# The first 20 feed-forward steps in a written order, the decay of chunk 1 moved onto q, and one chunk's PV in plain float32

## The chip, the cores and the metric

One core of a Trainium2 chip runs the program. The metric is the device time of one execution in microseconds (us). The kernel before takes 504.51 us in the median of three runs (504.18 to 506.27). Engines are named as in the profile: PE is TensorE (PEld its weight loads), DVE VectorE, ACT ScalarE, POOL GpSimd, SP the engine that issues most DMAs.

## The reference

An mLSTM attention over 768 positions (2 batches of 8 heads, head size 40), then two gated feed-forward layers on 1536 tokens of width 320 with an inner width of 1536, all in float32:

```python
for t in range(S):                                   # attention, state C, n, m
    m_new = np.maximum(f_gate[:, :, t] + m, i_gate[:, :, t])
    f_stab = np.exp(f_gate[:, :, t] + m - m_new)
    i_stab = np.exp(i_gate[:, :, t] - m_new)
    C = f_stab * C + i_stab * einsum('bhd,bhe->bhde', vt, kt)
    n = f_stab * n + i_stab * kt
    h_tilde = einsum('bhde,bhe->bhd', C, qt)
    y[:, :, t] = sigmoid(o_gate[:, :, t]) * h_tilde / max(|n . qt|, 1)
x = y.transpose(0, 2, 1, 3).reshape(1536, 320)
x = (sigmoid(x @ w_gate) * (x @ w_val)) @ w_out      # layer 1
xn = x / sqrt(mean(x * x) + 1e-6) * rms_g
g = xn @ w_gate2                                     # layer 2
out = (g * sigmoid(g) * (xn @ w_val2)) @ w_out2
```

## The kernel before

**Attention.** The 768 positions are six chunks of 128. For a chunk c and a batch b, `a_s` multiplies k and q, `a_p` multiplies the scores by a decay factor, `a_pv` multiplies them with v (the part of the output from inside the chunk), `a_inter` multiplies q with the masked state `cm` of the chunk before (the part from the state) and scales it by `te`, `a_u` updates the state, `a_h` adds the two parts, applies the sigmoid of the output gate and divides, and `a_x` transposes the result into `xT`. A float32 number for TensorE's faster type is held as a rounded high part and a low remainder: hence `xT` (high, low), the weights `wg` and `wo`, and `h` (high, low). The factors of chunks 0 and 1 come from matmuls, those of later chunks from a scan (`a_f`). The PV of chunk 2 and earlier is plain float32; from chunk 3 (`PB = 3`) on, the scores and v are split into three bfloat16 pieces each (`split3`, `a_v`), and each head takes three bfloat16 matmuls.

**Feed-forward.** A layer's inner width is cut into 12 weight tiles f. A step is one chunk (256 tokens in layer 1, 512 in layer 2) with one tile: `moe` or `moe2` does 16 matmuls into the bank `g`, a sigmoid on ACT and a product on DVE make `h`, and `moe_out` or `moe2_out` multiplies `h` with the output weights into the `o` banks. `ORDER` lists the 24 steps of chunks 0 and 1; then come 48 steps of chunks 2 to 5 and 36 of layer 2. A step's `moe_out` stands one step behind it for chunks 0 and 1, two behind for later chunks (`SKEW`).

**Weights.** Tile f comes in 64-bit form (960 numbers on 128 partitions) by `load_w` into one of two buffers `wraw`. `conv_w`, `conv_1` and `conv_2` make float32 of it: two ACT passes (or one, with a shift on DVE) and three DVE passes of 960, 640 and 320 columns. `split_w` makes `wg`: three ACT copies for the high parts, then the remainders: one 64x128 subtraction on POOL, one 128x512 subtraction on DVE (`go = 1`) or two 128x256 on POOL (`go = 0`), and another 64x128 on DVE (`low`). For chunks 0 and 1 the output weights stay plain float32 in `wf`; `split_o` splits them for later chunks.

**Order.** Each engine runs its own list of instructions in order, and waits for semaphores of the others. What the code emits in the prologue and in the first `NPIN = 8` steps is kept in the order of the code on each engine (`pin`); the rest is placed by a scheduler that goes by the code's order as priority. `early(i)` holds the attention work and the weight conversions that stand behind steps 0 to 3, `at(t, ...)` those of later steps. Two `wraw` buffers mean that the load of tile f + 2 waits for `conv_2` of tile f; SP issues loads in order, so what stands behind a waiting load waits too.

Of the kernel before, what the change touches and what calls it, by code (L numbers as in the profile page):

```python
# [19 lines left out]
L = 128  # L20
# [12 lines left out]
NPIN = 8  # L33
# [4 lines left out]
C2S = (8, 10)  # L38
XF = (0, 0, 0, 0, 0, 0, 0, 0, 0, 0, 0, 0)
LW = 9  # L40
FILL = (1, 3, 0, -3, 0, 0, 5)
ORDER = '000011110101010101010101'
C1S = (-4, -2)
EV1 = (-1, 4, 5, 0, 5, 3, 4, 5, 5, 6, 6, 7, 8)
EV2 = (0, 3, 3, 2, 4, 3, 3, 5, 5, 5, 5, 7, 7)
S0 = -4
CV = 5
SG1 = (0,) * NF
SG2 = (0, 0, 0, 0, 0, 0, 0, 0, 0, 0, 0, 0)
SP = 4  # L50
# [8 lines left out]
PB = 3  # L59
# [9 lines left out]
def mlstm_moe_kernel(ctx, tc, gate_if, gate_s, qk, qg, tok, w1, w2, rms_g, cst, out):  # L69
    nc = tc.nc  # L70
    pool = lambda name, bufs=1, **kw: ctx.enter_context(tc.tile_pool(name=name, bufs=bufs, **kw))
# [72 lines left out]
    def conv_w(f, tag="wc", lo_dve=0, both=True, sg_act=0, dve=False):  # L144
# [59 lines left out]
    def sub(eng, out, a, b):  # L204
        eng.tensor_tensor(out=out, in0=a, in1=b, op=ALU.subtract)  # L205
# [16 lines left out]
    def split_w(f, go=0, oo=0, both=True, eng=None):  # L222
# [12 lines left out]
        def low():  # L235
            sub(nc.vector, t[64:128, 0, 2, :], r[0:64], t[0:64, 0, 2, :])
# [39 lines left out]
    fd = dp.tile([U * (NC - LOGS), L], F32, name="fd")  # L276
    one = p2.tile([128, 8, E], F32, tag="hs", name="one").rearrange("p h e -> p (h e)").bitcast(BF16)[0:U, 0:S1]
# [154 lines left out]

    def a_inter(c, b, tag="a"):
# [3 lines left out]
        for g, (h0, n) in enumerate(GROUPS):  # L437
            nc.tensor.matmul(out=ps[:, h0 * E:(h0 + n) * E], lhsT=q[0:n * D, g, :], rhs=cm[0:n * D, g, 0:n * E], start=True, stop=True)  # L438
# [3 lines left out]
    def a_pv(c, qd, tag="a", fill=0):  # L442
        b, o = qd // 2, 4 * (qd % 2)
        if c >= PB:
            ps = pv_t[c, qd] = bank(tag)
        else:
            if o == 0:
                pv_t[c, b] = bank(tag)
            ps = pv_t[c, b]
        p = p_t.pop((c, qd))  # L450
        v = v_of(c, b)
        for i in range(4):
# [8 lines left out]
            nc.tensor.matmul(out=ps[:, (o + i) * E:(o + i + 1) * E], lhsT=p[:, i, :], rhs=v[:, o + i, :], start=True, stop=True)  # L461
# [171 lines left out]
    at(10, lambda: nc.gpsimd.tensor_scalar(out=rmsg, in0=rmsg, scalar1=2.0 ** -16, scalar2=None, op0=ALU.mult))  # L633
# [5 lines left out]
    for f in range(NF):  # L639
        t = pos[1, 0, f]  # L640
        at(NF * NAT + f - 1, split_o, f, O1[f])
        if f >= 6:
            at(t - LW, load_w, w1, f)
        if f >= 4:
            at(t - CV, keep.add, f)
            at(t - CV, conv_w, f, "wc", L1[f], True, SG1[f])
            at(t - SP, split_w, f, G1[f], O1[f])
# [3 lines left out]
        assert t + 1 < 72 + f and SP < CV  # L651
# [53 lines left out]
    load_qk(1, 1)  # L705
    gates_r2()
# [25 lines left out]
    keep.update((0, 1, 2, 3))  # L732
# [6 lines left out]
    a_o(0, 1)  # L739
    a_u(0, 0, "a")  # L740
    load_tok(1, 0)
# [5 lines left out]
    x = x_t.pop(0).rearrange("p b h d -> p b (h d)")  # L747
    a_u(0, 1, "o0")
    load_w(w1, 2)
    load_tok(1, 1, False)  # L750
    gates_r5b()
    idle = bank("o3")
    busy(idle, *[512] * 3)
    xT_dup(xT[1, 0], 0, x[:, 0], "o2", False)()
    conv_w(1, "wc", 1, False)
    a_s(1, 0, "aa")
    xT_dup(xT[1, 0], 1, x[:, 1], idle)
    rest()
    gates_r5c()
    conv_1(1)  # L760
    conv_2(1)
    load_w(w1, 3)
    p.tensor_copy(out=ident4, in_=ident.unsqueeze(1).to_broadcast([128, 4, L]))
# [108 lines left out]
    done = 0  # L872
    after = ExitStack()

    def early(i):

        if i == 0:
            split_w(1, 1)
            a_s(1, 1, ("o2", "o3"))
            for qd in range(4):  # L880
                a_k(1, qd)
            a_p(1, 0)
            a_p(1, 1)
            conv_w(2)
        elif i == 1:
            a_inter(1, 0)
            load_qg(1, 1)
            load_w(w1, 4)
            split_w(2, 1)
            a_p(1, 2, p2.tile([128, 4, L], F32, tag="ft", name="p"))  # L890
            a_p(1, 3, p2.tile([128, 4, L], F32, tag="ft", name="p"))
            a_o(1, 0)
            a_o(1, 1)
            a_pv(1, 0)
            a_pv(1, 1)
            a_u(1, 0)
            conv_w(3)
            load_w(w1, 5)
        elif i == 2:
            a_h(1, 0)  # L900
            split_w(3, 1)
            a_inter(1, 1, "o2")
            a_pv(1, 2, "o3")
            a_pv(1, 3, "o3")
            a_u(1, 1, "a")
            a_x(1, 0, "a")
            a_h(1, 1)
        elif i == 3:
            a_x(1, 1, "o2")

    assert min(ev) >= 0, min(ev)
    for i in range(len(seq) + SKEW):
# [9 lines left out]
        if 0 <= i < len(seq):  # L922
# [3 lines left out]
            if i < NPIN:  # L926
                early(i)
        while 0 <= i and done < len(seq) and done <= i - (SKEW if seq[done][0] == 1 and seq[done][1] >= NAT else 1):
            layer, c, f = seq[done]
            (moe_out if layer == 1 else moe2_out)(c, f)  # L930
            done += 1
# [84 lines left out]
```

## Time and profile before

| | us |
|---|---|
| median of three runs | 504.51 (504.18 to 506.27) |
| the profiled execution | 505.04 |
| its span, from the first to the last instruction | 503.2 |
| PE busy | 485.2 |
| DVE / ACT / POOL busy | 303.1 / 222.5 / 210.0 |
| mean granted TensorE clock | 0.989 |

The page's time slices show PE at nine tenths or more from a quarter of the span to the end, except in a stretch before three fifths of it. The three other engines are busiest in the first quarter and again in that stretch, where the second layer's weights come in. A matmul's record can overlap that of the next, so a sum of records is more than the time they take; where a cost is needed, starts of neighbouring records are compared.

### The profile page before, as it was taken

How to read it: one execution, taken by the hardware profiler on the slowest of the kernel's cores; microseconds unless marked ns; L12 is line 12 of the kernel's file. 1: busy time of each engine (PE TensorE's matmuls, PEld its weight loads, DVE VectorE, ACT ScalarE, POOL GpSimd, SP SyncE). 2: the span in 40 equal slices, each digit the busy share in tenths (PEclk: the TensorE clock that was granted, in tenths of full speed). 3: DMA queues.
4: the chain of work that ended last, by engine and by line, in shares of the span. 5: the costliest groups of instructions: out<-in, count | busy, mean ns of one | idle time of the engine just before them, and what ended most of it. 6: DMA issues, size and time to landing. Idle time of an engine off the chain costs nothing.

```text
span 503.2 us, 8423 instructions
## 1 busy us (share of the span) xinstructions
PE 485.2 (96%) x3264; PEld 434.8 (86%) x3266; DVE 303.1 (60%) x564; ACT 222.5 (44%) x485; POOL 210.0 (42%) x238
## 2 busy tenths in 40 slices
PE   8988989899999999999999889999999999999997
PEld 5877869678899999999999778988888888888886
DVE  6899594993679586596779986622352222432223
ACT  3764653553434543455578666322252222432122
POOL 2733385451256364354249996332213222132221
PEclk9998989899999999999999999999999999999999
DMA  7763736721123232023444412000010000100001
GB/s 233 250 208 116 239 108 251 253 98 40 61 64 84 80 85 82 1 67 108 158 158 156 158 66 92 1 0 1 0 54 0 1 0 1 53 2 0 1 0 52
DMA packets 12557, 42.58 MB, mean 85 GB/s; under 512 B 1590, under 2 KB 4870, under 8 KB 12518
## 3 DMA queue, kind: packets, MB, share of 16 engines
q1 hardware_dynamic: 12278, 41.84, 24.8%
q8 instruction: 25, 0.41, 0.3%
q10 hardware_dynamic: 240, 0.22, 0.2%
q14 instruction: 14, 0.11, 0.1%
HBM read 40.05 MB, written 2.00 MB: 84 GB/s over the span
## 4 chain that ended last, share of the span: by engine, by line
PE 65%; DVE 5%; DMA 4%; POOL 3%; issue 2%; ACT 1%; POOLq 0%; ACTq 0%
PE g L804 13%; PE a L804 13%; PE o L856 12%; PE g L786 11%; PE o L831 6%; PE o L786 4%; DMA wraw<-in_w_dram 4%; PE o L828 2%; POOL h L205 1%; POOL wg L205 1%; DVE wg L205 1%; PE a L392 1%; PE a L457 1%; PE a L438 1%; PE a L470 1%
## 5 line engine op out<-in xcount | busy, mean ns | idle before, releaser
L786 PE MATMUL g<-xT,wg 128*128 128x256 f32 x912 | 131.2, 293 | 1.1 <-ACT gb L338 0.4
L786 PEld LDWEIGHTS g<-xT,wg 128*128 128x128 f32 x912 | 118.2, 193 | 7.2 <-issue 1.7
L205 POOL TENSOR_TENSOR ft<-p,fb 128x512 fp32r<-128x512 f32 x35 | 45.2, 1293 | 130.6 <-ACT fb L813 130.5
L807 DVE TENSOR_TENSOR p<-p,g 128x512 f32<-128x512 f32 x36 | 24.5, 686 | 91.0 <-ACT p L806 91.0
L205 POOL TENSOR_TENSOR h<-sig,h 128x256 fp32r<-128x256 f32 x48 | 44.9, 938 | 57.2 <-ACT h L795 56.0
L831 PE MATMUL o<-wo,h 128*128 128x320 f32 x288 | 52.0, 313 | 3.9 <-POOL h L205 3.8
L856 PE MATMUL o<-wo,fb 128*128 128x320 f32 x288 | 52.9, 310 | 0.0
L804 PE MATMUL g<-xT,wg 128*128 128x512 f32 x180 | 50.7, 393 | 0.1
L813 ACT ACTIVATE fb<-p 128x512 fp32r<-128x512 f32 (+1 forms) x37 | 22.8, 620 | 60.7 <-DVE p L812 54.5
L806 ACT ACTIVATE p<-g 128x512 f32<-128x512 f32 x36 | 21.3, 596 | 62.9 <-PE g L804 59.8
L831 PEld LDWEIGHTS o<-wo,h 128*128 128x128 f32 x288 | 43.2, 189 | 6.2 <-POOL h L205 5.1
L804 PE MATMUL a<-xT,wg 128*128 128x512 f32 x180 | 47.6, 390 | 0.0
L856 PEld LDWEIGHTS o<-wo,fb 128*128 128x128 f32 x288 | 45.6, 188 | 2.0
L804 PEld LDWEIGHTS a<-xT,wg 128*128 128x128 f32 x180 | 33.7, 188 | 6.9
L812 DVE TENSOR_TENSOR p<-p,a 128x512 f32<-128x512 f32 (+1 forms) x37 | 24.6, 671 | 22.6 <-PE a L804 22.5
L804 PEld LDWEIGHTS g<-xT,wg 128*128 128x128 f32 x180 | 32.5, 188 | 5.5 <-ACT xT L515 0.4
L828 PE MATMUL o<-wf,h 128*128 128x320 f32 x96 | 34.1, 481 | 2.9 <-DVE h L791 2.9
L786 PE MATMUL o<-xT,wg 128*128 128x256 f32 x240 | 34.7, 290 | 0.0
L788 ACT ACTIVATE sig<-g 128x256 f32<-128x256 f32 x57 | 21.5, 377 | 26.8 <-PE g L786 23.5
L205 POOL TENSOR_TENSOR wg<-wc,wg 128x256 fp32r<-128x256 f32 (+1 forms) x30 | 22.8, 771 | 24.2 <-ACT wg L209 22.4
L167 ACT ACTIVATE wraw<-wraw 128x960 f32<-128x960 f32 x23 | 25.2, 1097 | 14.1 <-DMA wraw<-in_w_dram 13.9
L856 PE MATMUL o<-wo,ft 128*128 128x320 f32 x144 | 31.4, 309 | 0.0
(258 smaller groups left out, 863.5 us busy)
## 6 DMA issues: line engine op xcount, KB each, us to landing
wraw<-in_w_dram SPq DMA_DIRECT2D x24, 960.0 KB
tok<-in_tok_dram SPq DMA_DIRECT2D x12, 488.0 KB
fb<-fd SPq DMA_DIRECT2D x16, 256.0 KB
raw<-in_qk_dram SPq DMA_DIRECT2D x24, 160.0 KB
out_dram<-xn SPq DMA_DIRECT2D x12, 160.0 KB
qg<-in_qg_dram SPq DMA_DIRECT2D x10, 180.0 KB
rmsg<-in_rms_g_dram SPq DMA_DIRECT2D x1, 160.0 KB
cs<-in_cst_dram ACTq DMA_DIRECT2D x1, 136.5 KB
```

The source lines that it names most:

```text
L167: nc.scalar.activation(out=hi.bitcast(F32), in_=hi.bitcast(F32), func=AF.Copy, scale=2.0 ** -111)
L205: eng.tensor_tensor(out=out, in0=a, in1=b, op=ALU.subtract)
L786: nc.tensor.matmul(out=g[:, m, :], lhsT=w[:, m, ws, :], rhs=x[xs // 3][:, xs % 3, :], start=(i == 0), stop=(i == 7))
L788: nc.scalar.activation(out=sg, in_=g[:, 0, :], func=AF.Sigmoid, scale=2.0 ** -8)
L804: nc.tensor.matmul(out=g[m], lhsT=w[:, m, ws, :], rhs=x[xs // 3][:, xs % 3, :], start=(i == 0), stop=(i == 7))
L806: nc.scalar.activation(out=sg, in_=g[0], func=AF.Sigmoid, scale=2.0 ** -8)
L807: nc.vector.tensor_tensor(out=sg, in0=sg, in1=g[0], op=ALU.mult)
L812: nc.vector.tensor_tensor(out=sg[:, n], in0=sg[:, n], in1=g[1][:, n], op=ALU.mult)
L813: nc.scalar.activation(out=h[0][:, n], in_=sg[:, n], func=AF.Copy)
L828: nc.tensor.matmul(out=o, lhsT=h[:, n], rhs=w, start=(f == 0), stop=(f == NF - 1))
L831: nc.tensor.matmul(out=o, lhsT=h[:, hs, n], rhs=w[:, ws, :], start=(f == 0 and i == 0), stop=(f == NF - 1 and i == 2))
L856: nc.tensor.matmul(out=o, lhsT=h[hs][:, n], rhs=w[:, ws, :], start=(f == 0 and i == 0), stop=(f == NF - 1 and i == 2))
```

## The change

The prologue and the first 20 steps (`NPIN = 20`) stand in a written order. Two tables, `pre` and `post`, list what is emitted ahead of and behind each step's `moe`; they take the place of `early` and of the entries of `at` for chunk 2 and for the weight tiles of layer 1. In parts:

- Chunk 1: `load_q1` loads q into the (still unused) weight buffers of tiles 10 and 11, `load_e` reads the decay `er` back from DRAM as a broadcast, and `a_q` multiplies q by it on POOL. The state part and PV then accumulate in one bank, so that scaling by `te` and adding the two parts fall away, and `a_h0` finishes the chunk.
- Chunk 3's PV is plain float32 (`PB = 4`), with 8 matmuls for a batch instead of 24, and without `split3` and the splitting of v.
- Weights: tile 1's shift moves from DVE to ACT (`conv_z`). For tiles 2 to 11 of layer 1 the remainders are all made on POOL (`go = 0`); `low` goes to POOL wherever `go = 0`, in layer 2 as well (tiles 2, 3, 6, 7, 9 and 11).
- The output of steps 0 to 2 stands behind the attention work of the same step; `gates_r5b` uses one bank; three dummy matmuls go; the scaling of `rmsg` moves from POOL to ACT; `split_o` and all that is not pinned stands behind step 19.

```diff
-NPIN = 8
+NPIN = 20
-C2S = (8, 10)
+C3S = (19, 25)
-ORDER = '000011110101010101010101'
+ORDER = '000011110101010101010011'
-PB = 3
+PB = 4
@@ split_w
         def low():
-            sub(nc.vector, t[64:128, 0, 2, :], r[0:64], t[0:64, 0, 2, :])
+            sub(nc.vector if go else nc.gpsimd, t[64:128, 0, 2, :], r[0:64], t[0:64, 0, 2, :])
@@ chunk 1
+        nc.sync.dma_start(out=ed, in_=er[:, 0:L])
+    def load_e(b):
+        t = eq_t[b]
+        for i in range(3):
+            n = 3 if i < 2 else 2
+            rows = ed[8 * b + i:8 * b + i + 3 * (n - 1) + 1:3, :]
+            nc.sync.dma_start(out=t[D * i:D * i + D, 0:n], in_=rows.unsqueeze(0).to_broadcast([D, n, L]))
+    def a_q(b):
+        q, t = qg_t[1, b], eq_t.pop(b)
+        for n, g in ((120, slice(0, 2)), (80, slice(2, 3))):
+            nc.gpsimd.tensor_tensor(out=q[0:n, g], in0=q[0:n, g], in1=t[0:n, g], op=ALU.mult)
@@ a_inter
-            nc.tensor.matmul(out=ps[:, h0 * E:(h0 + n) * E], lhsT=q[0:n * D, g, :], rhs=cm[0:n * D, g, 0:n * E], start=True, stop=True)
+            nc.tensor.matmul(out=ps[:, h0 * E:(h0 + n) * E], lhsT=q[0:n * D, g, :], rhs=cm[0:n * D, g, 0:n * E], start=(c > 1 or g == 0), stop=(c > 1))
+        if c == 1:
+            pv_t[c, b] = ps
+            return
@@ the written order
+    pre = {
+        0: [(a_p, 1, 0), (tile_b, 1)],
+        1: [(tile_d, 1), (tile_b, 2)],
+        2: [(a_h0, 0, 1), (tile_b, 3)],
+        3: [(tile_b1, 4), (a_x, 1, 1, "o2"), (tile_b2, 4)],
+    }
+    post = {
+        0: [(a_p, 1, 1), (tile_c, 1, 1), (tile_a, 2), (conv_z, 2), (a_s, 1, 1, ("o2", "o3")), ...
...
+        19: [(a_u, 2, 1), (lambda: nc.scalar.activation(out=rmsg, in_=rmsg, func=AF.Copy, scale=2.0 ** -16),)],
```

`tile_a` is ACT's part of a tile's conversion, `tile_b` DVE's and the load of tile f + 2, `tile_c` the split.

On DVE, at the start of the steps, stood this (`wc<-wraw` and `wf` are a tile's conversion, `wg` its remainders, `p` scores times decay, `h` a step's product, `hs<-a,te` the state part scaled):

```order
L205 TENSOR_TENSOR xT<-o_387,xT 128x3x128
L176 TENSOR_SCALAR wc<-wraw 128x960
L205 TENSOR_TENSOR xT<-o_383,xT 128x3x128
L205 TENSOR_TENSOR wg<-wc,wg 64x128
...
L791 TENSOR_TENSOR h<-sig,g 128x256
L205 TENSOR_TENSOR wg<-wc,wg 128x2x256
L205 TENSOR_TENSOR wg<-wc,wg 64x128
L401 TENSOR_TENSOR p<-a,d_195 128x512 x2
...
L791 TENSOR_TENSOR h<-sig,g 128x256
L440 TENSOR_TENSOR hs<-a,te 128x336
L205 TENSOR_TENSOR wg<-wc,wg 128x2x256
L205 TENSOR_TENSOR wg<-wc,wg 64x128
```

In the changed kernel the same place reads so:

```order
L208 TENSOR_TENSOR xT<-o_362,xT 128x3x128
L208 TENSOR_TENSOR xT<-o_403,xT 128x3x128
L406 TENSOR_TENSOR p<-a,d_196 128x512
...
L814 TENSOR_TENSOR h<-sig,g 128x256
L406 TENSOR_TENSOR p<-a,d_196 128x512
L208 TENSOR_TENSOR wg<-wc,wg 128x2x256
L208 TENSOR_TENSOR wg<-wc,wg 64x128
...
L814 TENSOR_TENSOR h<-sig,g 128x256
L406 TENSOR_TENSOR p<-o_473,d_197 128x512
L406 TENSOR_TENSOR p<-o_474,d_197 128x512
```

The gaps hold the passes of a tile's conversion. The shift, the remainders of tiles 2 and 3 and the scaling of `hs` are gone from DVE; the first scores times decay stand ahead of tile 1's conversion.

On POOL, near the end of layer 1, the remainders of layer 2's weights stand between the steps' `h`. Before:

```order
L205 TENSOR_TENSOR h<-sig,h 128x256 x2
L205 TENSOR_TENSOR wg<-raw,wg 128x256 x2
L205 TENSOR_TENSOR wg<-raw,wg 64x128
L205 TENSOR_TENSOR h<-sig,h 128x256
L205 TENSOR_TENSOR wo<-wc,wo 128x320
L205 TENSOR_TENSOR wo<-tok,wo 128x320
```

After:

```order
L208 TENSOR_TENSOR h<-sig,h 128x256
L208 TENSOR_TENSOR wo<-wc,wo 128x320
L208 TENSOR_TENSOR wg<-raw,wg 128x256 x2
L208 TENSOR_TENSOR wg<-raw,wg 64x128 x2
L208 TENSOR_TENSOR wo<-tok,wo 128x320
L208 TENSOR_TENSOR h<-sig,h 128x256
```

Between two `h` there now stand six subtractions in a row, where it was three and then two; one of them is the `low` that was on DVE.

## Rows read from the trace of the kernel before

**Rows 1.** Busy us by stretch, engine by engine, then granted clock, DMA share, GB/s
```profile
26.00:52.00 26.00, 22.92 (x163) 19.71 (x164) 25.11 (x50) 13.84 (x28) 7.28 (x12) 0.93 0.42 145
52.00:138.00 86.00, 80.57 (x546) 70.59 (x545) 60.48 (x98) 42.07 (x87) 40.15 (x48) 0.96 0.45 153
138.00:223.00 85.00, 85.00 (x766) 82.48 (x766) 62.42 (x142) 39.01 (x101) 45.60 (x58) 1.00 0.22 62
223.00:300.00 77.00, 72.76 (x578) 68.60 (x575) 64.45 (x113) 51.19 (x122) 49.14 (x50) 1.00 0.38 131
300.00:503.00 203.00, 199.59 (x1045) 175.51 (x1044) 70.94 (x122) 62.18 (x124) 54.73 (x48) 1.00 0.06 20
```

**Rows 2.** What PE waited for over the whole span: us in total, times, longest
```profile
PE o L831 <- POOL h L205: 3.8, 3, 1.8
PE o L828 <- DVE h L791: 2.9, 2, 2.3
PE a L438 <- DVE p L401: 2.0, 1, 2.0
PE a L553 <- DVE x L499: 1.7, 1, 1.7
```

**Rows 3.** A stretch of 2 us, columns as in rows 1
```profile
46.00:48.00 2.00, 2.00 (x6) 1.41 (x5) 1.93 (x7) 1.98 (x2) 0.99 (x2) 0.50 0.02 4
```

**Rows 4.** DVE's groups, 24 to 52 us: busy us, mean ns, idle before
```profile
L205 DVE TENSOR_TENSOR wg<-wc,wg 128x512 fp32r<-128x512 f32 x3 | 2.1, 685 | 0.0
L205 DVE TENSOR_TENSOR wg<-wc,wg 64x128 fp32r<-64x128 f32 x4 | 1.5, 378 | 0.1
L176 DVE TENSOR_SCALAR wc<-wraw 128x960 int32<-128x960 int32 x1 | 1.1, 1120 | 0.0
L440 DVE TENSOR_TENSOR hs<-a,te 128x336 f32<-128x336 f32 x1 | 0.5, 500 | 0.0
L490 DVE TENSOR_TENSOR hs<-a,hs 128x336 f32<-128x336 f32 x1 | 0.5, 494 | 0.0
```

**Rows 5.** POOL's groups of weight remainders, 60 to 303 us
```profile
L205 POOL TENSOR_TENSOR wg<-wc,wg 128x256 fp32r<-128x256 f32 x12 | 12.9, 1095 | 0.1
L205 POOL TENSOR_TENSOR wg<-wc,wg 64x128 fp32r<-64x128 f32 x9 | 4.2, 461 | 10.6 <-ACT wg L209 10.2
L205 POOL TENSOR_TENSOR wg<-tok,wg 64x128 fp32r<-64x128 f32 x3 | 2.6, 873 | 0.2
```

**Rows 6.** PE in order of time at two PVs: start, us, instruction, count
```profile
40.13 1.92 PE L461 MATMUL o<-tok,p 128*128 128x42 f32 x16
41.87 0.81 PE L470 MATMUL a<-tok,kk 128*120 128x126 f32 x6
...
139.61 1.02 PE L457 MATMUL a<-wraw,wc 128*128 128x42 bf16 x22
140.47 2.16 PE L786 MATMUL g<-xT,wg 128*128 128x256 f32 x16
```

**Rows 7.** POOL in order of time while layer 2's weights are split
```profile
281.72 3.27 POOL L205 TENSOR_TENSOR wg<-raw,wg 128x256 fp32r<-128x256 f32 x3 [1.01 <-ACT wg L209]
...
285.89 1.30 POOL L205 TENSOR_TENSOR wo<-wc,wo 128x320 fp32r<-128x320 f32 x1
287.14 1.80 POOL L205 TENSOR_TENSOR wo<-tok,wo 128x320 fp32r<-128x320 f32 x1
288.90 1.65 POOL L205 TENSOR_TENSOR h<-sig,h 128x256 fp32r<-128x256 f32 x1
```

**Rows 8.** PE in order of time, the starts of two neighbouring steps
```profile
54.40 2.32 PE L786 MATMUL g<-xT,wg 128*128 128x256 f32 x16
...
57.39 2.32 PE L786 MATMUL g<-xT,wg 128*128 128x256 f32 x16
```

**Rows 9.** One small DVE subtraction beside POOL work
```profile
93.09 2.49 DVE L205 TENSOR_TENSOR wg<-wc,wg 64x128 fp32r<-64x128 f32 x1
```

**Rows 10.** ACT waiting for a weight tile of layer 1
```profile
88.14 1.12 ACT L167 ACTIVATE wraw<-wraw 128x960 f32<-128x960 f32 x1 [2.51 <-DMA wraw<-in_w_dram]
```

More of the change, by code (lines that the diff above doesn't have):

```diff
@@ L276, in mlstm_moe_kernel @@
     fd = dp.tile([U * (NC - LOGS), L], F32, name="fd")
+    ed = dp.tile([U, L], F32, name="ed")
     one = p2.tile([128, 8, E], F32, tag="hs", name="one").rearrange("p h e -> p (h e)").bitcast(BF16)[0:U, 0:S1]
@@ L446, in a_pv @@
         else:
-            if o == 0:
+            if o == 0 and c != 1:
                 pv_t[c, b] = bank(tag)
@@ L731, in mlstm_moe_kernel @@
     a_pv(0, 1, "a")
[L732 removed]
+    keep.update(range(NF))
     conv_w(0, "wc", 2, False, 0, True)
@@ L747, in mlstm_moe_kernel @@
     x = x_t.pop(0).rearrange("p b h d -> p b (h d)")
+    low = xT_dup(xT[1, 0], 0, x[:, 0], "o2", False)
     a_u(0, 1, "o0")
     load_w(w1, 2)
+    load_e(0)
     load_tok(1, 1, False)
[L751 to L755, printed above, removed]
+    load_e(1)
+    gates_r5b("g")
+    low()
+    xT_dup(xT[1, 0], 1, x[:, 1], "o3")
     a_s(1, 0, "aa")
-    xT_dup(xT[1, 0], 1, x[:, 1], idle)
     rest()
[L759 to L763, printed above, removed]
+    a_q(0)
+    a_q(1)
+    conv_z(1)
     def pin(first):
@@ L871, in mlstm_moe_kernel, with ft_tile @@
     hst = {}
-    done = 0
     after = ExitStack()
[L875 to L909, printed above, removed]
+    def ft_tile():
+        return p2.tile([128, 4, L], F32, tag="ft", name="p")
@@ new lines, in tile_a, with tile_b, tile_b1, tile_b2 @@
+    def tile_a(f):
+        conv_w(f, "wc", 3, False)
+    def tile_b(f):
+        tile_b1(f)
+        tile_b2(f)
+    def tile_b1(f):
+        if f in tops:
+            conv_z(f)
+        conv_1(f)
+    def tile_b2(f):
+        conv_2(f)
+        if f + 2 < NF:
+            load_w(w1, f + 2)
+    lows = {}
+    def tile_c(f, go=0):
+        low = split_w(f, go, 0, not go)
+        if go:
+            lows[f] = low
+    def tile_d(f):
+        if f in lows:
+            lows.pop(f)()
+    pre = {
[4 more added lines that the diff above has]
+    }
@@ L911, in mlstm_moe_kernel, with do, out_steps @@
+    for f in range(4, NF):
+        pre.setdefault(2 * f - 3, []).append((tile_d, f))
+    def do(todo):
+        for fn, *args in todo:
+            fn(*(x() if x is ft_tile else x for x in args))
+    def out_steps(i):
+        nonlocal done
+        while 0 <= i and done < len(seq) and done <= i - (0 if done < 3 else SKEW if seq[done][0] == 1 and seq[done][1] >= NAT else 1):
+            layer, c, f = seq[done]
+            (moe_out if layer == 1 else moe2_out)(c, f)
+            done += 1
     assert min(ev) >= 0, min(ev)
@@ L925, in mlstm_moe_kernel @@
             (moe if layer == 1 else moe2)(c, f)
[L926 to L931, printed above, removed]
+        if i >= 3:
+            out_steps(i)
+        do(post.get(i, ()))
+        out_steps(i)
     after.close()
```

109 lines of the change are left out of this document (69 added, 40 removed).

## The prediction

> **What bounds the kernel now.** I read the page's time slices first, then PE's waits, then the busy time by stretch, then the engines in order of time where PE waits. From 300 us to the end PE is busy in 199.59 of 203.00 us, the rest being the tail behind the last matmul, and in 138 to 223 us it is busy in 85.00 of 85.00 us at a granted clock of 1.00 [rows 1]: there only less PE work saves time. It is fed badly in three stretches. From 26 to 52 us it is idle for 26.00 - 22.92 = 3.08 us while DVE is busy in 25.11 of 26; from 52 to 138 us idle for 86.00 - 80.57 = 5.43 us; from 223 to 300 us idle for 4.24 us [rows 1]. The first two have also a mean granted clock of 0.93 and 0.96 [rows 1]: after waits of 1.7 to 2.3 us [rows 2] PE goes on at the lower level (1.2 of 2.4 GHz) for some us, as at 46 us with a granted clock of 0.50 [rows 3]. Rows 2 name who is late: DVE with a product, with the scores and with x in the first two, and in the third POOL with `h`, three times, 3.8 us. So the front hangs on DVE's order and load, the third stretch on POOL's.
>
> **The sum.** It is made against the profiled execution, 505.04 us (span 503.2 and 1.8 around it), and put on the median of the runs, 504.51.
>
> *Prologue and steps 0 to 3 (26 to 52 us).* To be had: 3.08 us of waits and, from the clock, 0.07 x 26 = 1.8 us, together 4.9. DVE loses one shift of 1.12 us, two scalings of 0.50 and two additions of 0.49, two 128x512 remainders of 0.685 and two 64x128 of 0.378 [rows 4]: 5.2 us out of 25.11. So DVE, with no gap before, gets one of about 5 us, and x of chunk 1 comes before PE asks for it or less than 1 us later. The 1.7 us wait for x [rows 2], and the clock that falls after it, go. What is late next is the remainder of tile 2, now on POOL: 2 x 1.095 + 2 x 0.461 = 3.1 us behind ACT's copies [rows 5], against some 1.1 us on DVE, and PE's fifth matmul of the step reads the last of them. I leave 0.9 us of wait there and 0.7 us at x of chunk 1, so the credit is 4.9 - 1.6 = 3.3. Bounds: all goes, 4.9; or both tiles' longer chains (2 x 2.0) show in full and the clock falls again, a loss of 1.
>
> The decay on q is four POOL multiplications ahead of tile 1's remainder. No row has their shape; a 64x128 subtraction took 0.46 and a 128x256 one 1.1 [rows 5], so four take 1.8 to 4.4, and since three quarters of them are nearer to the smaller in columns I take 2.5. They end about 30 us, and tile 1's remainder is asked for about 31: hidden by the first step's 16 matmuls (2.32 us [rows 8]) and the scores behind it. If their DRAM round trip is late (six broadcasts stand on SP behind two token loads and one weight load), PE waits at the state part up to 2 us; these 2 stand in the bound. The two q loads replace two that are gone; ACT takes the 1.1 us pass of tile 1 and the scaling of `rmsg`, with 13.84 us busy out of 26 and 42.07 out of 86 [rows 1]. The three dummy matmuls stood in a wait; their going is counted at nothing.
>
> *Steps 4 to 23 (52 to 138 us).* To be had: 5.43 us of waits and 0.04 x 86 = 3.4 us of clock, 8.8 in all. The 2.0 us wait for scores and the 2.3 us one for a product [rows 2] come from DVE's order: the wanted instruction stood behind weight conversions and scans. In the written order each `h` has at most a tile's conversion and one scan ahead of it, and its PE step starts two groups later; steps are 57.39 - 54.40 = 2.99 us apart [rows 8]. DVE loses the 128x512 remainders of tiles 9 to 11 and all `low`; POOL makes seven tiles at 3.1 us, 22 us, in a stretch in which it is busy in 40.15 of 86 us [rows 1], and of that its eight `wo` remainders leave for later. A weight tile is asked for every second step, 6 us, and has its conversion four steps ahead. I credit 6.4 and leave 2.4 (waits that an order by hand keeps). Bounds: 8.8 and 2.
>
> *What leaves this stretch* is the splitting of the output weights, pressed into some ten steps after step 19. ACT's 39.01 and POOL's 45.60 of 85 us [rows 1] cover it, and chunk 3 gives back ACT, DVE and POOL work there; without that cover it would cost a wait of about one `h`, 1 to 2 us, and it is part of the range.
>
> *Chunk 3's PV.* 22 of a batch's 24 bfloat16 matmuls take 140.47 - 139.61 = 0.86 us, so 24 take 0.94; the float32 ones of a batch take 41.87 - 40.13 = 1.74 us [rows 6]. PE pays 0.8 us for each of two batches where it has no slack: +1.6. All that ACT, DVE and POOL save in chunk 3 lies beside a PE that does not wait, and saves nothing.
>
> *Layer 2's weights (223 to 300 us).* The stretch moves earlier as a whole, since its first load waits for a buffer that PE's own progress frees. Inside it POOL gets `low` of tiles 2 and 3 (0.46 each) and of 6 and 7 (0.87 by the nearest row) before PE's last wait [rows 5]: 2.7 us on the engine that PE waits for. Also the order: between two `h` now stand both `wo` (1.30 and 1.80 us) and the `wg` group of 3.27 [rows 7] plus a `low`, some 7 us, where 3.1 us between two `h` already went with a wait of 1.8 [rows 2, 7]. Against it DVE gets free of four subtractions, and the `h` that is late had two steps, 6 us, of room. I charge 2.3. Bounds: 6 (both gaps show), and a gain of 1 (DVE's relief shows).
>
> Sum: -3.3 - 6.4 + 1.6 + 2.3 = -5.8. From 505.04 that is 499.2, and on the median **498.7 us**.
>
> **Where a page speaks against it.** Beside other POOL work a DVE subtraction of 64x128 took 2.49 us [rows 9] and 0.378 in the mean elsewhere [rows 4]: DVE stood still while POOL worked. The Trainium skill (SBUF — State Buffer, section Terms) says that the two share a pair of memory ports which one instruction holds to its end while the other is blocked. By that, moving remainders from DVE to POOL frees no time while both read memory; the trace agrees in rows 9. The time that this would give is the first rival.
>
> **Rivals.**
>
> 1. *DVE and POOL take turns, and the written order only shifts the waits.* If DVE stands still in every POOL remainder, steps 0 to 3 gain nothing (5.2 us off DVE, 2 x 3.1 us of POOL and 2.5 for q in its place), and of the 8.8 half is kept: 4.4. Then -4.4 + 1.6 + 2.3 = -0.5: 504.0. For it: rows 9. Against it: POOL is busy in only 7.28 of 26 us [rows 1], and in 24 to 52 us the 64x128 subtraction's mean is 0.378 [rows 4], so most of them went undisturbed.
>
> 2. *Nothing is late any more.* 4.9 + 8.8, less 1.6, with the third stretch as before: 504.5 - 12.1 = 492.4. For it: PE's own work is short enough, and 138 to 223 us shows that a full PE is possible. Against it: POOL's new load in the third stretch.
>
> 3. *Slower: the weights' loads become the bound.* A tile's load goes out only after the conversion of the tile two before it, and with 19 steps fixed nothing can be pulled ahead of ACT when it waits. ACT waited 2.51 us for a tile [rows 10]. If each of tiles 5 to 11 comes that late with the next sigmoid behind it on ACT, PE loses 7 x 2.5 = 17.5 us, against 9.7 of credit and with 3.9 of charges: 504.5 + 11.7 = 516. It decides once a load takes longer than the three steps, 9 us, from its issue to its use. Against it: in 52 to 138 us DMA is busy 0.45 of the time [rows 1], so there is room.
>
> **How the numbers follow.** What a measurement of this kernel can tell from no change is 0.5%, 2.5 us: 502.0 to 507.0. The forecast has 0.64, with its own range of 495 to 502; rival 1 has 0.15, rival 2 0.14, rival 3 0.07. Faster is nearly all of the forecast and rival 2, 0.76; same is rival 1, 0.15; slower is rival 3 and the outer end of the POOL charge, 0.09. The range takes in rival 2's edge and rival 1: 492.5 to 504.5.
>
> **What would show it.** Right: in 26 to 138 us of the changed kernel's time no PE wait over 1.5 us, a granted clock of 0.98 or more, and layer 1's first split output about 9 us earlier; PV of chunk 3 as 16 float32 records with 1.7 us to what follows; PE's waits for POOL's `h` near the end of layer 1 at 5 to 7 us in total, up from 3.8. Wrong: PE waits for `wg` from POOL in steps 1 to 3 for more than 3 us in all; ACT waiting for `wraw` in steps 5 to 18; or waits for `h` over 9 us, which would give back the front's gain.

## The result, and the profile after

The changed kernel takes 501.13 us in the median of 7 runs (497.9 to 513.47), the kernel before 504.78 us in 7 runs beside it. The ratio is 0.9916, with a 95% interval of 0.989 to 0.9943: faster by 0.8%. The prediction was 498.7 us, with 492.5 to 504.5 as its range. The profiled execution took 500.93 us, with a span of 499.1, against 505.04 and 503.2 before.

Some executions of most kernels here run at a lower clock throughout; the ratios leave them out and the medians do not, so where the two disagree, as in e5, the ratio counts.

What PE waited for over the span of the changed kernel, as in [rows 2]: us in total, times, longest.

```profile
PE o L854 <- POOL h L208: 4.3, 3, 2.8
PE o L851 <- DVE h L814: 1.9, 1, 1.9
PE a L397 <- issue: 1.6, 1, 1.6
...
PE o L582 <- DVE x L541: 0.5, 1, 0.5
```

The wait for the scores (2.0) is gone, that for chunk 1's x has shrunk (1.7, now 0.5), and one for a product of DVE's stays (2.3, now 1.9). One is new, 1.6 us ahead of the score matmuls of `a_s`. POOL's `h` costs 4.3 where it cost 3.8.

Busy time by stretch, with the columns of [rows 1]; the borders behind 52 us are moved with the work. The first row is a stretch of 2 us.

```profile
24.00:26.00 2.00, 2.00 (x18) 1.53 (x18) 0.56 (x1) 1.52 (x5) 1.71 (x4) 0.57 0.95 343
...
26.00:52.00 26.00, 24.87 (x184) 22.11 (x183) 21.52 (x40) 14.24 (x28) 15.42 (x22) 0.90 0.44 149
52.00:126.00 74.00, 70.47 (x486) 61.34 (x485) 50.97 (x78) 34.43 (x68) 37.62 (x56) 0.98 0.51 162
...
223.00:296.00 73.00, 68.68 (x542) 65.68 (x542) 59.42 (x95) 47.81 (x111) 48.01 (x49) 0.98 0.36 126
```

PE's idle time, read as stretch less busy, is 1.13 us in 26 to 52 (before 3.08), 3.53 in 52 to 126 (before 5.43 up to 138) and 4.32 in 223 to 296 (before 4.24) [rows 1]. Against that, the clock column is worse in two places: 0.90 instead of 0.93 in 26 to 52, and 0.57 just ahead of it. A clock of 0.90 over 26 us costs about 0.10 x 26 = 2.6 us, 0.57 over 2 us another 0.9. The front's waits went as planned and most of the gain was given back there in clock.

Two places explain the waits that are left. The first, DVE in order of time around 88 us:

```profile
85.02 1.64 DVE L193 SCALAR_TENSOR_TENSOR wc<-wraw,wc 128x960 int32<-128x960 int32 x1 [0.56 <-ACT wc L184]
86.69 2.00 DVE L205 SCALAR_TENSOR_TENSOR wc<-wraw,wc 128x640 int32<-128x640 int32 x1
88.61 0.48 DVE L205 SCALAR_TENSOR_TENSOR wf<-wraw,wc 128x320 int32<-128x320 int32 x1
89.01 0.49 DVE L518 TENSOR_TENSOR hs<-a,hs 128x336 f32<-128x336 f32 x1
...
94.32 1.16 DVE L193 SCALAR_TENSOR_TENSOR wc<-wraw,wc 128x960 int32<-128x960 int32 x1
95.51 0.82 DVE L205 SCALAR_TENSOR_TENSOR wc<-wraw,wc 128x640 int32<-128x640 int32 x1
```

and PE there:

```profile
87.52 0.48 PE L397 MATMUL a<-raw 40*128 40x128 f32 x2
89.61 1.13 PE L397 MATMUL a<-raw 40*128 40x128 f32 x14 [1.60 <-issue]
```

The profile puts the 1.60 us down to "issue". What PE stands for is a bank: `a` is held by PV until the addition of L518 has read it, that addition stands in the written order behind tile 9's conversion (the first three rows), and PE goes on 0.6 us behind the addition's start. The conversion was itself late: its first two passes took 1.64 and 2.00 us beside a POOL that ran without a gap from 84.96 to 88.01, and 1.16 and 0.82 for the next tile (the last two rows). These 1.66 us are about PE's wait, so by this estimate a DVE held up beside POOL is behind it, as in the second place.

The second is ahead of step 20's output, directly behind the last written step. DVE:

```profile
110.11 1.39 DVE L359 TENSOR_TENSOR_SCAN ft<-fb,ident 128x512 f32<-128x512 f32 x1
111.42 4.49 DVE L521 TENSOR_TENSOR x<-x,hs 128x320 f32<-128x320 f32 x1
...
115.90 0.41 DVE L814 TENSOR_TENSOR h<-sig,g 128x256 f32<-128x256 f32 x1
```

POOL in the same time:

```profile
109.73 0.69 POOL L506 TENSOR_TENSOR cm<-C,cs 120x252 f32<-120x252 f32 x1 [2.57 <-DVE C L505]
110.37 1.28 POOL L507 TENSOR_TENSOR cm<-C,cs 80x84 f32<-80x84 f32 x1
111.61 0.75 POOL L420 TENSOR_TENSOR vv<-tok,tg 128x336 f32<-128x336 f32 x1
112.32 0.46 POOL L436 TENSOR_TENSOR kk<-tok,ft 128x160 f32<-128x160 f32 x1
112.74 0.87 POOL L208 TENSOR_TENSOR wo<-wf,wo 128x320 fp32r<-128x320 f32 x1
113.57 0.75 POOL L420 TENSOR_TENSOR vv<-tok,tg 128x336 f32<-128x336 f32 x1
114.28 0.46 POOL L436 TENSOR_TENSOR kk<-tok,ft 128x160 f32<-128x160 f32 x1
114.70 0.86 POOL L208 TENSOR_TENSOR wo<-wf,wo 128x320 fp32r<-128x320 f32 x1
116.14 0.86 POOL L208 TENSOR_TENSOR wo<-wf,wo 128x320 fp32r<-128x320 f32 x1 [0.58 <-ACT wo L212]
```

The addition L521 takes 0.49 us at other places. Here it takes 4.49: POOL runs eight instructions with no gap from 109.73 to 115.56, and the addition ends 0.35 us after POOL's first pause. The product `h` that PE wants is queued two places behind it, so PE waits 1.93 us:

```profile
116.36 2.48 PE L851 MATMUL o<-wf,h 128*128 128x320 f32 x4 [1.93 <-DVE h L814]
```

Behind that wait the clock is low, and the output's four matmuls take 2.48 us, where with the clock up they take 1.3.

The same stood in the kernel before. The `h` that PE waited 2.3 us for there came directly behind the subtraction of [rows 9], which took 2.49 us beside POOL where the mean in 24 to 52 us is 0.378 [rows 4]:

```profile
95.60 0.42 DVE L791 TENSOR_TENSOR h<-sig,g 128x256 f32<-128x256 f32 x1
```

### The profile page after: what moved, and what is told of

Its sections match the earlier page's. It is cut to its first block, busy times and chain, and to the rows that moved or that the text cites. A ratio compares the mean times of both kernels' runs of the same rounds, so it can differ in the third digit from the quotient of the medians.

```text
span 499.1 us, 8348 instructions
## 1 busy us (share of the span) xinstructions
PE 484.7 (97%) x3246; PEld 436.3 (87%) x3247; DVE 284.0 (57%) x519; ACT 217.6 (44%) x475; POOL 218.6 (44%) x264
## 5 line engine op out<-in xcount | busy, mean ns | idle before, releaser
L809 PE MATMUL g<-xT,wg 128*128 128x256 f32 x912 | 128.4, 292 | 0.6 <-POOL wg L208 0.6
L830 DVE TENSOR_TENSOR p<-p,a 128x512 f32<-128x512 f32 x36 | 24.5, 687 | 90.9 <-ACT p L829 90.9
L208 POOL TENSOR_TENSOR wg<-wc,wg 64x128 fp32r<-64x128 f32 (+1 forms) x53 | 37.3, 715 | 31.9 <-ACT wg L212 27.1
L827 PE MATMUL a<-xT,wg 128*128 128x512 f32 x180 | 50.8, 394 | 0.1
L829 ACT ACTIVATE p<-a 128x512 f32<-128x512 f32 x36 | 21.3, 598 | 62.2 <-PE a L827 58.4
L827 PE MATMUL g<-xT,wg 128*128 128x512 f32 x180 | 47.4, 390 | 0.0
L827 PEld LDWEIGHTS a<-xT,wg 128*128 128x128 f32 x180 | 32.5, 188 | 5.5 <-ACT xT L544 0.4
L835 DVE TENSOR_TENSOR p<-p,g 128x512 f32<-128x512 f32 (+1 forms) x37 | 24.6, 672 | 21.3 <-PE g L827 21.2
L851 PE MATMUL o<-wf,h 128*128 128x320 f32 x96 | 31.3, 449 | 1.9 <-DVE h L814 1.9
L809 PEld LDWEIGHTS o<-xT,wg 128*128 128x128 f32 x240 | 31.1, 192 | 0.1
```

The costliest lines, as they stand in the source:

```text
L809: nc.tensor.matmul(out=g[:, m, :], lhsT=w[:, m, ws, :], rhs=x[xs // 3][:, xs % 3, :], start=(i == 0), stop=(i == 7))
L827: nc.tensor.matmul(out=g[m], lhsT=w[:, m, ws, :], rhs=x[xs // 3][:, xs % 3, :], start=(i == 0), stop=(i == 7))
L829: nc.scalar.activation(out=sg, in_=g[0], func=AF.Sigmoid, scale=2.0 ** -8)
L830: nc.vector.tensor_tensor(out=sg, in0=sg, in1=g[0], op=ALU.mult)
L835: nc.vector.tensor_tensor(out=sg[:, n], in0=sg[:, n], in1=g[1][:, n], op=ALU.mult)
L851: nc.tensor.matmul(out=o, lhsT=h[:, n], rhs=w, start=(f == 0), stop=(f == NF - 1))
```

## The experiments

Twelve kernels were run, each against runs of the kernel before on the same chip.

**e1, the changed kernel again**, beside the next three as their yardstick. No edit.

> The changed kernel once more, as the yardstick for the others of this call. By the theory of the clock (the small matmuls of the prologue, without the three dummy matmuls, let the granted clock fall to 0.5 for some 7 us before the first step): most of the runs at 501 us, and single ones near 498 us with a mean clock near 0.993, where that fall does not come. By the rival (the spread has another cause): the time varies without the mean clock varying with it.

500.69 us, ratio 0.9895 (0.9847 to 0.9943). Its six executions run from 497.18 us at a mean clock of 0.997 to 520.42 at 0.949, each lower clock with a longer time, so the rival is out; that the missing dummy matmuls are the cause is not shown by this. Its profiled execution is 2.8 us shorter than the first (span 496.3), and it is worth setting the two side by side, because the instructions are the same, the longer waits too, and the clock is not. One wait of 0.50 us, for `eq`, is in e1 and not in the first, where PE came there later. PE's waits of e1 between 24 and 126 us (one of 0.60 us for split weights is left out):

```profile
29.17 0.90 PE L463 MATMUL a<-cm,eq 120*128 120x126 f32 x6 [0.50 <-POOL eq L456]
...
44.85 0.41 PE L582 MATMUL o<-cs,x 128*128 128x128 f32 x2 [0.53 <-DVE x L541]
...
87.03 1.33 PE L397 MATMUL a<-raw 40*128 40x128 f32 x14 [1.60 <-issue]
...
115.28 1.34 PE L851 MATMUL o<-wf,h 128*128 128x320 f32 x4 [1.93 <-DVE h L814]
```

and three stretches of e1, columns as above:

```profile
24.00:32.00 8.00, 7.50 (x72) 6.57 (x72) 6.33 (x10) 5.78 (x12) 4.85 (x10) 1.00 0.80 256
...
85.00:95.00 10.00, 8.40 (x55) 7.61 (x55) 6.93 (x13) 3.81 (x7) 3.00 (x6) 0.83 0.67 208
...
116.00:120.00 4.00, 4.00 (x29) 3.27 (x28) 3.36 (x6) 1.32 (x3) 0.88 (x1) 1.00 0.00 0
```

In the first execution the clock was low in 24 to 31 us and after 116 us, and full after 88. In e1 it is full in 24 to 32 and after 116, and 0.83 after the wait at 87. From the wait for x to the one for the bank both executions take 42.18 us; from there to the wait for `h` 26.75 us in the first and 28.25 in e1. So the same wait of 1.6 us was followed by a low clock in one execution and not in the other, and the low clock cost 28.25 - 26.75 = 1.5 us there.

**e2, dummy matmuls.** The prologue gets dummy matmuls back, 2 x 512 columns ahead of each half's transposes.

```
+    idle = bank("o3")
+    busy(idle, 512, 512)
...
+    busy(idle, 512, 512)
```

> The change, with four dummy matmuls of 512 columns back in the prologue: two in PE's 0.46 us wait for x and two ahead of the second half's transposes, about 0.5 us of work on PE's path. Theory (clock): the granted clock stays at 1.00 from 24 to 32 us; the first step's 16 matmuls take 2.2 to 2.5 us in place of 3.7, and of the 2.8 us lost there 1.5 to 2.5 come back, since the decay on q and tile 1's remainder on POOL, which end at 33 us, are next to be late: 498.5 to 499.5 us. Rival (PE is held in this place by its operands, and the slow records only show that): no gain, 501 to 501.5.

498.36 us, ratio 0.9861 (0.9827 to 0.9896), with a full clock in 20 to 126 us in its profile. Its interval overlaps that of e1. The five executions in its ratio have mean clocks of 0.990 to 0.997; of the eleven in the ratios of the result and of e1 four reach 0.990. e7 and e10 below take up the question.

**e3, layer 2's `low` back on DVE.**

```
-            sub(nc.vector if go else nc.gpsimd, t[64:128, 0, 2, :], r[0:64], t[0:64, 0, 2, :])
+            sub(nc.vector if go or f in second else nc.gpsimd, t[64:128, 0, 2, :], r[0:64], t[0:64, 0, 2, :])
```

> The change, with the low remainder of layer 2's tiles back on DVE (as before the change); layer 1 as changed. Theory (these subtractions lengthen POOL's chain between two h): PE's waits for h near the end of layer 1 fall from 4.3 us to 3 to 4, and the clock does not fall there: 1 to 2 us less than the change, 499.5. Rival (the order between the two h counts, or DVE gives back what it gained): waits of 4 us or more and a time within 0.7 us of the change.

499.22 us, ratio 0.9861 (0.9817 to 0.9906). PE's waits for POOL's `h` in e3:

```profile
PE o L857 <- POOL h L210: 2.6, 2, 1.8
```

That is 1.7 us less than in the change, and the longest is 1.8 where it was 2.8, so `low` on POOL is what made the third stretch's wait longer. The clock fell behind the shorter wait too: in 223 to 296 us it is 0.98 in e3 as in the change. The time fell by less than the medians can tell (1.5 us, intervals overlapping).

**e4, chunk 3's PV in bfloat16 as before.** This part of the change alone is undone.

```
-PB = 4
+PB = 3
```

> The change, with chunk 3's PV in three bfloat16 pieces again (as before the change). Theory (PE is full there, and a batch's PV costs 0.8 us more in float32): 1.6 us less than the change, 499.5. Rival (chunk 3's splitting loads ACT, DVE and POOL in the same steps as the output weights' splitting, which now stands there too): new PE waits between 110 and 150 us that eat the gain or more, 501 to 504.

504.63 us, ratio 0.9999 (0.9958 to 1.0041): with this one constant put back, the whole gain is gone. Of the theories the one lost that counted the float32 PV as a charge. DVE of e4 where the change has its 4.49 us addition:

```profile
111.08 6.01 DVE L521 TENSOR_TENSOR x<-x,hs 128x320 f32<-128x320 f32 x1
```

The end of POOL's run there:

```profile
114.36 0.82 POOL L208 TENSOR_TENSOR hs<-vv,wraw 128x336 f32<-128x336 f32 x1
115.14 0.86 POOL L208 TENSOR_TENSOR wo<-wf,wo 128x320 fp32r<-128x320 f32 x1
115.96 0.78 POOL L208 TENSOR_TENSOR wraw<-hs,wraw 128x336 bf16<-128x336 f32 x1
```

PE's wait that follows in e4:

```profile
117.55 2.50 PE L851 MATMUL o<-wf,h 128*128 128x320 f32 x4 [3.45 <-DVE h L814]
```

and the stretch of e4 around it, columns as above:

```profile
116.00:126.00 10.00, 8.45 (x30) 6.64 (x31) 5.66 (x11) 1.83 (x4) 2.80 (x5) 0.54 0.01 5
```

Splitting v into bfloat16 pieces puts two more subtractions (`hs<-vv,wraw`, `wraw<-hs,wraw`) into POOL's run. It now ends at 116.74, the addition 0.35 us later, PE waits 3.45 us instead of 1.93, and goes on at a mean clock of 0.54 up to 126 us, where e1 had 1.00 in 116 to 120. All six executions of e4 have mean clocks of 0.988 or less, so the loss in clock is not that of one profile.

**e5, one line of the written order turned round**, against the 1.6 us for the bank.

```
-        13: [(tile_b, 9), (a_h, 2, 0)],
+        13: [(a_h, 2, 0), (tile_b, 9)],
```

> Step 13 of the written order puts a_h(2,0) ahead of tile 9's conversion; all else as in the change. Theory (the 1.6 us that PE waits at 88 us in a_s(2,1) for bank a is the place of a_h behind the conversion, and is paid in full, since PE is late from there on): that wait is gone, DVE's hs add stands 2 to 3 us earlier against moe(12), no new PE wait over 0.8 us before 110 us, and at equal clock the span is 1.6 us shorter (about 496.5 us at a clock of .993). Rival (whatever comes first on DVE beside POOL is stretched, so the conversion that now comes later makes moe(14) or (15) wait for its tile): a wait of 1 to 2 us for xn or h after step 14 and a span within 0.5 us of the change's.

Median 506.46 us, ratio 0.9852 (0.9807 to 0.9898), against e1's 0.9895. In its profiled execution the clock was 0.50 in 20 to 32 us, and the matmuls of `a_s` that waited for the bank start at 100.89 us instead of 87.52; in 52 to 126 us the clock was 1.00. The wait for the bank is gone there, and a new one for a product stands 10 us behind its place:

```profile
111.10 1.34 PE L851 MATMUL o<-wf,h 128*128 128x320 f32 x4 [0.59 <-DVE h L814]
```

e10 below, with the same edit and a full clock in 84 to 100 us, has the same wait, 0.58 us, again 10 us behind. So of 1.60 us about one, 1.60 - 0.59, is kept. The intervals of e1 and e5 overlap; the traces tell them apart, the times do not.

**e6, the written order to step 23.**

```
-NPIN = 20
+NPIN = 23
```

> The written order holds for 23 steps instead of 20, so the planner takes over 9 us later. Theory (the 1.9 us wait for h(20) at 114 to 116 us comes from POOL's run of cm, vv, kk, wo, vv, kk, wo that the planner puts directly behind the last written step, while DVE's add of x stands still for 4.5 us): the wait at 114 us is gone, the add of x is back below 1 us there; 1.9 us and the low clock that followed it (about 1 us) come back, 2 to 3 us in all at equal clock elsewhere, unless the same run of POOL returns at step 23, when the wait comes back 9 us later and the time is as in the change. Rival (it is the evictions of chunk 3 that fall due there, not POOL's run): a wait for h of 1.5 to 2.5 us stays within 110 to 120 us whatever the order.

498.81 us, ratio 0.9868 (0.9849 to 0.9887): 1.9 us under e1, with intervals that overlap. The same addition in e6:

```profile
112.14 0.49 DVE L521 TENSOR_TENSOR x<-x,hs 128x320 f32<-128x320 f32 x1
```

and POOL, whose last instruction ahead of it ends at 111.39:

```profile
110.65 0.74 POOL L420 TENSOR_TENSOR vv<-tok,tg 128x336 f32<-128x336 f32 x1
124.12 0.56 POOL L866 TENSOR_TENSOR ss<-ss,mhalf 128x1 f32<-128x1 f32 x1 [12.73 <-DVE ss L865]
```

With POOL silent the addition takes 0.49 us and the wait for `h` is gone; in its place PE waits 0.77 us for `xT` and 0.58 for scores. Three lengths of one instruction now stand beside three runs of POOL: 0.49 with none, 4.49 with a run that ends at 115.56, 6.01 with one that ends at 116.74. The rival (chunk 3's evictions fall due there whatever the order) is out.

**e7, the kernel before without its dummy matmuls.**

```
-    busy(idle, *[512] * 3)
```

> The kernel before without its three dummy matmuls of 512 columns ahead of the first half's transposes, and nothing else. Prediction on record (they stood in a wait and their going costs nothing): same time, within 0.5 us, clock of 20 to 32 us as before. Theory now (they kept the granted clock up for the first feed-forward step; without them it can fall to .50 for some microseconds there): in executions where it falls, a_s and moe(0) take 2 to 3 us longer and the time is 2 to 3 us longer than before; the median lies 0 to 3 us above the kernel before. If the clock stays over .95 in 24 to 32 us, the fall in the change's profile was not from the dummies alone.

504.89 us, ratio 0.9983 (0.9958 to 1.0007), and in its profile a clock of 1.00 from 24 to 32 us. In the kernel before, the dummies have no effect that shows, as the prediction had it.

**e8, the kernel before with float32 PV in chunk 3.**

```
-PB = 3
+PB = 4
```

> The kernel before with chunk 3's PV in plain float32 (PB=4), and nothing else: that part of the change alone. Prediction on record: 16 float32 matmuls are 0.9 to 1.7 us longer on PE than the bfloat16 ones, so about 1.6 us slower than before. Theory now (with bfloat16 DVE and POOL split two more operands per head beside wo's, and PE waits for them, as e4 showed in the changed order: 4 to 5 us): 0 to 4 us faster than before, with the p splits of chunk 3 gone from DVE. If it is slower by 1 to 2 us, the gain of float32 in e4 comes only with the new order, in which those splits stand in a different place.

504.32 us, ratio 0.998 (0.996 to 1.0). PE at the first of the two PVs:

```profile
136.59 1.88 PE L461 MATMUL a<-vv,p 128*128 128x42 f32 x16
138.29 0.36 PE L786 MATMUL g<-xT,wg 128*128 128x256 f32 x1
```

A batch takes 138.29 - 136.59 = 1.70 us, against the 0.94 counted from [rows 6]. The term was measured well, 0.76 us a batch. The kernel is all the same not slower by 1.6 us but faster by 0 to 2. What pays it back in this kernel the trace doesn't settle: its waits for POOL's `h` are 2.7 us instead of 3.8, those for DVE about as before.

**e9 and e10, the mends together**, with and without the dummies: e3's, e5's and e6's edits in both, e2's in e9 alone.

> Four edits together: dummy matmuls of 2 x 512 columns ahead of both halves' transposes in the prologue, the layer-2 weights' low part on DVE, a_h(2,0) ahead of tile 9's conversion, the written order to step 23. If the losses are separate places they add: from the change at a clock of .993 (498 us) 1.6 us (wait at 88 us) + 2 (wait at 114 us) + 1.7 (layer-2 weights) are taken off, about 493 us; median 492.5 to 494.5, ratio to before .974 to .980. If one loss only hands its time to the next wait (the rival: DVE is what is short, and whatever is freed it waits again a little later), 496 to 498 us. Clock of 24 to 32 us over .95, and the executions' mean clocks all at .99 or over.

> As e9, without the dummy matmuls. Theory (without them the granted clock can fall in 24 to 32 us, in some executions and not in others, which costs 2 to 3 us each time): at equal clock as e9; some executions at .986 and below, which e9 does not have, and a median 0.5 to 3 us above e9's. Rival (the dummies do nothing; the clock falls by chance, with them or without): the two have the same clocks and the same median within 0.7 us.

e9: 495.65 us, ratio 0.9802 (0.9773 to 0.9831). e10: 495.95 us, ratio 0.9811 (0.9783 to 0.9839). Both beat the kernel before by 2% and the change by about 1% (0.9802 / 0.9895 = 0.991). The time lies between the two expectations, 492.5 to 494.5 and 496 to 498. PE's waits in e10 from 80 to 126 us:

```profile
95.50 1.34 PE L854 MATMUL o<-wf,h 128*128 128x320 f32 x4 [0.58 <-DVE h L817]
113.64 1.16 PE L400 MATMUL a<-raw 40*128 40x128 f32 x14 [0.77 <-DVE xT L210]
115.37 1.58 PE L466 MATMUL a<-cm,qg 120*128 120x126 f32 x6 [0.58 <-DVE p L409]
```

So of the 1.60 + 1.93 = 3.53 us of waits taken out here, 0.58 + 0.77 + 0.58 = 1.93 came back in three small ones: the losses don't simply add, since DVE is late a little further on. e9 and e10 differ by 0.3 us: the dummies have no effect that shows here. That does not clear them for the change: e10's profile has a clock of 1.00 in 24 to 52 us and its five mean clocks are 0.990 or more, so there may have been no fall to mend. Why the clock was low in 24 to 31 us in some executions of the changed prologue (the first, e6, e11, e12) and full in others (e1, e3, e4, e10), all without dummies and e12 with its own edit, stays open.

**e11, the written order to step 7 only.**

```
-NPIN = 20
+NPIN = 8
```

> The change with the written order for its first 8 steps only; the planner places steps 8 to 19 as it finds best, with the change's other two parts in place. By the prediction's term for steps 4 to 23 (6.4 us of credit, by number of steps 12 of 20 of it) it is 3 to 4 us slower than the change, with waits of PE for h and for the split weights between 64 and 112 us. Rival (what gains is PV in float32 and the order of the first 8 steps, the planner would do as well later): within 1 us of the change.

500.85 us, ratio 0.9904 (0.9876 to 0.9933): not to be told from the change. In its trace PE waits, behind step 7, for `wo`, and three times for `h`:

```profile
70.09 1.50 PE L489 MATMUL a<-vv,p 128*128 128x42 f32 x12 [0.86 <-POOL wo L208]
81.17 2.12 PE L851 MATMUL o<-wf,h 128*128 128x320 f32 x4 [2.50 <-DVE h L814]
94.58 1.34 PE L851 MATMUL o<-wf,h 128*128 128x320 f32 x4 [1.10 <-DVE h L814]
102.53 1.34 PE L851 MATMUL o<-wf,h 128*128 128x320 f32 x4 [1.00 <-DVE h L814]
```

Together 5.5 us, where the change waits 1.60 + 1.93 = 3.5 in that part. The twelve later steps of the written order are worth 2 us of waits, not the 3 to 4 of the first theory.

**e12, the decay on q on DVE instead of POOL.**

```
-            nc.gpsimd.tensor_tensor(out=q[0:n, g], in0=q[0:n, g], in1=t[0:n, g], op=ALU.mult)
+            nc.vector.tensor_tensor(out=q[0:n, g], in0=q[0:n, g], in1=t[0:n, g], op=ALU.mult)
```

> The four multiplications that put the decay on chunk 1's q run on DVE instead of POOL; all else as in the change. Prediction on record: on POOL they take 2.5 us and are hidden. Theory: on DVE four of them take 2 to 2.6 us, in the stretch 26 to 36 us in which DVE has almost no gap, and the first stands still until its data lands (POOL waited there 1.8 to 2.5 us); so x of chunk 1 comes 2 to 4 us later, PE waits 2 to 4 us more before 50 us and the time is 2 to 4 us longer than the change (502 to 505 us; ratio to before .993 to 1.0). Rival (DVE and POOL take turns anyway, so it makes no difference on which of them the work stands): within 1 us of the change.

503.83 us, ratio 0.9955 (0.9927 to 0.9982), by the ratios 2 to 3 us slower than the change (0.9916 and 0.9895), as the theory had it, but with intervals that overlap. DVE of e12:

```profile
27.51 0.61 DVE L456 TENSOR_TENSOR eq<-eq 120x256 f32<-120x256 f32 x2
29.50 0.62 DVE L456 TENSOR_TENSOR eq<-eq 120x256 f32<-120x256 f32 x2 [1.38 <-DMA eq<-ed]
30.05 0.68 DVE L406 TENSOR_TENSOR p<-a,d 128x512 f32<-128x512 f32 x1
```

The first scores times decay now stand 2.5 us behind the start of q's, half of it in a wait for data. The clock in this profile was low before that place, so the trace doesn't split the 2 to 3 us between the two.

## Why the prediction was right, and where it was not

The total was right within its range; the terms were not all, and their errors cancel in part, so that the total came so near is in part luck. Profile against profile it lost 505.04 - 500.93 = 4.1 us where 5.8 was forecast. By idle time and clock, as read above, the front gives 1.95 - 0.8 - 0.9 = 0.25 us, steps 4 to 23 3.8, and the third stretch takes 1.6 back: 2.45 us. The other 1.65 us lie in PE's own busy time, though the PV of chunk 3 adds 2 x 0.76 there (e8): other work of PE's got some 3 us shorter, and which is not shown.

- **Prologue and steps 0 to 3, credit 3.3.** The idle time fell from 3.08 to 1.13 us, and in e1 to 26.00 - 24.37 = 1.63, with a clock of 1.00; there the term is 1.5 of waits and 1.8 of clock, 3.3 us. The mechanism and the size hold in e1, where the clock stays up. In the first profile they don't: the clock took back some 3 us.
- **The three dummy matmuls, counted at nothing.** Their going was the first suspect for that low clock. e7 (0.9983) and e9 against e10 (0.3 us) found nothing, while the mean clocks of e2 are mostly higher than those of the change, so for the changed prologue the term is neither refuted nor shown. The step that failed is another: the prediction took a full clock as the result of no waits, and in four of eight profiled executions of this prologue it was not full.
- **The q decay on POOL, 2.5 us and hidden.** In e1 the four take 1.42 + 1.22 = 2.64 us and PE waits 0.50 for them; in the first profile they take 3.87, and PE, at the lower clock, does not wait. Two of the four have 256 columns and two 128, not three quarters the smaller: by the prediction's own rows that is 2 x 1.1 + 2 x 0.46 = 3.1 us. On DVE the time is 2 to 3 us longer, at the edge of what the runs can tell (e12). So hidden but for half a us, and sized a little low.
- **Steps 4 to 23, credit 6.4.** Idle time fell from 5.43 to 3.53 us and clock loss from 3.4 to 0.02 x 74 = 1.5: 3.8 us. The step that failed is "each `h` has at most a tile's conversion and one scan ahead of it". It counts what stands ahead of `h` and not how long it takes beside POOL: at 111 us one addition ahead of `h` stood still through POOL's whole run, which the planner set right behind the last written step (e6). And it looks at `h` alone: at 88 us the addition that frees a bank stood behind a conversion (e5). Where 2.4 us were left for waits, 8.8 - 3.8 = 5.0 stayed; the lower bound, 2, was nearer than the 6.4 taken.
- **Chunk 3's PV, a charge of 1.6.** PE does pay 0.76 us a batch (e8). The step that failed is "all that ACT, DVE and POOL save in chunk 3 lies beside a PE that does not wait, and saves nothing". In the changed order two of POOL's subtractions stand in the run that holds DVE, and bfloat16 costs 4 us (e4). The sign was wrong: taking this constant back loses the whole gain, and in the kernel before it brings 0 to 2 us (e8).
- **Layer 2's weights on POOL, a charge of 2.3.** The waits for `h` are 4.3 us instead of 3.8, and the longest moved from 1.8 to 2.8; with `low` on DVE they are 2.6, so `low` alone costs 1.7 (e3). PE's idle time in the stretch is up by only 0.1 us, but its clock is 0.98 instead of 1.00, 0.02 x 73 = 1.5 us: the fall follows the longest wait (0.50 in 278 to 280 us). So 1.6 was paid in this profile. That the change brings the part in clock is not shown: e3, with a longest wait of 1.8 us, has 0.98 as well, and e12, with 2.8, has 1.00.
- **Rivals.** That DVE and POOL take turns was given 0.15 as a whole-kernel story. As such it is out: it has 504.0 us and a front that gains nothing, and in e1 the front gained 3.3 though POOL's busy time in 26 to 52 us rose from 7.28 [rows 1] to 16.73. As a mechanism it is the largest loss left, at 111 us and by the estimate above at 88. It was in the kernel before too, in the wait of 2.3 us; the prediction had [rows 9] and put that wait down to the order alone. The weights' loads never became the bound: ACT, which waited up to 2.5 us for them [rows 10], does not wait for `wraw` between 52 and 126 us.
- **Signs named in advance.** No wait over 1.5 us in 26 to 138: missed, 1.60 and 1.93. A clock of 0.98: met in 52 to 126 us, missed in 26 to 52 (0.90). 1.7 us for a PV of chunk 3: met, 152.80 - 151.10. Waits for `h` of 5 to 7 us: 4.3. Layer 1's first split output 9 us earlier: it starts at 141.03 us, and at 142.47 before, only 1.4 us, since the work between is ordered differently too; this sign was badly chosen. Of the signs of being wrong none came.

## What to carry to other kernels

When work is moved off DVE onto POOL, look for the places where POOL then runs without a pause: a DVE addition that reads two SBUF operands took as long as the run here, and what counts is who is queued behind it. Judge an edit on an engine that seems to have slack by undoing it alone: here undoing the constant that lengthened PE's work lost the whole gain. A hand-written order should end where the automatic one has nothing piled up; the seam is the first place to look at.

## What the runs showed of the hardware

- A DVE addition of 128x320 with both operands in SBUF took 0.49 us beside an idle POOL, 4.49 and 6.01 beside unbroken runs of POOL, each time ending 0.35 us after POOL's first pause. An addition with one operand in PSUM (L518 at 109.69 us, 0.49 us) and POOL's `cm` beside it (0.69, as in e6) did not hold each other. It goes the other way too: POOL's 80x84 instruction of `cm` took 1.28 us while DVE's scan ran, and 0.36 in e6, where it did not; in the kernel before, its 120x252 one took 2.23 us from 90.80 us on, beside four DVE instructions in a row, though its record starts ahead of theirs. The Trainium skill (SBUF — State Buffer, section Who interferes with whom) says that a DVE instruction with two SBUF inputs contends with a GpSimd instruction that reads SBUF, and that the one that starts first blocks the other. The trace agrees for one instruction, and shows more: between two POOL instructions without a gap the waiting DVE one didn't get its turn, six times in a row in the changed kernel.
- After a PE wait of 1.6 or 1.9 us the granted clock went to its lower level (1.2 of 2.4 GHz) in one execution and stayed up in another of the same program, with the same waits to 0.01 us: 0.50 in 88 to 90 us of e1 and 1.00 there in the first profile, 0.54 in 118 to 120 us of the first profile and 1.00 there in e1. Behind the 1.6 us one that was worth 1.5 us, about as much as the wait itself.
